# Token softmax in halves ahead of the state's reads, 1/rms spread by column transposes, and twelve weight products moved from GpSimd to VectorE

## The chip, the cores and the metric

The kernel runs on one core of a Trainium2 chip. The core has five engines with a queue each: TensorE (PE; its weight loads are listed apart as PEld), VectorE (DVE), ScalarE (ACT), GpSimd (POOL) and SyncE (SP), which issues most of the transfers. Each queue is worked off in order. The metric is the device time of one execution in microseconds; the kernel before takes 912.96 us (median of three runs, 911.79 to 913.95).

## The reference

The first part is a recurrent cross attention with B, H, S, Ns, D = 8, 8, 512, 32, 64; its result is reordered to 8 x 544 rows of 512 numbers. The second part is a SwiGLU feed-forward with d_ff = 1536, behind an RMS norm.

```python
scores = scale * np.matmul(x, state.transpose(0, 1, 3, 2))
scores = scores - scores.max(-1, keepdims=True)
a = np.exp(scores)
a /= a.sum(-1, keepdims=True) + 1e-09
xread = np.matmul(a, state)
# the same with scores2 = scale * state @ x^T gives sread = a2 @ x
return np.concatenate([xread, sread], axis=2).astype(np.float32)
...
rms = np.sqrt(np.mean(x * x, axis=-1, keepdims=True) + 1e-06)
xn = x / rms * rms_g
g = xn @ w_gate
silu = g * (1.0 / (1.0 + np.exp(-g)))
val = xn @ w_val
return (silu * val @ w_out).astype(np.float32)
```

The softmax over the 32 states, one for each token and head, is called the token softmax here; the one over the 512 tokens is the state softmax.

## The kernel before

**Weights.** The three matrices come as float64 and are made float32 on the chip, in 18 pieces of 1 MB: 12 of gate and val (pieces 0 to 11), 6 of w_out (12 to 17). `load_piece` loads a piece into one of four raw buffers, `to_float32` converts it in eight instructions: L151, L156, L157 and L159 on DVE, L153, L154 and L155 on ACT, and the last product, L162, on POOL. `ready(n)` asks for the first n pieces.

**Attention.** `attention(b)` is a generator that a `yield` cuts into 20 steps. For a batch it loads the state, transposes x (L209, copied by L210), makes the scores (L217), copies them to SBUF (L225), does the state softmax (L226 to L234), transposes its weights (L241) and reads x with them (L249), asks for the next batch's x (L258 and L87), then does the token softmax (L266 to L286), transposes its result (L294), and reads the state with it (L304) only to obtain the sum of squares for the norm (L307). `inverse_rms` raises that sum to the power -1/2 on POOL (L173, L175), and `along` spreads the result over the partitions: DVE multiplies it into a diagonal (L181), PE multiplies that by ones (L184). L311 scales the softmax weights by it. They lie in `aT_s`, the only thing of a token's read that is kept: `make_v` multiplies the state by the weights (L345, copied by L352), and the hidden layer then is `aT_s` by that product.

**Batch 0** is done with plain products: `hidden` (L371) for 12 blocks m, two for each pair of gate and val pieces, with L376 on ACT and L377 and L379 on DVE; then `project_as_ready` (L457), 48 products, four for each m, each pair of m needing one piece of w_out. Attention(1) runs a few steps at a time in between. Behind it `weight_sums` (L487) makes sums of w_out's blocks.

**Batches 1 to 7** use seven products in place of eight: `hidden_seven` (L409; L419, L421, L426 and L434 on ACT; L424, L428, L430, L435, L439, L444 and L446 on DVE) for six pairs, with two steps of attention(b+1) behind each pair, and `project_seven` (L500, copies L520, sums L525, and L533 and L542) with up to five steps at each of four places. In batch 7 the steps are those of `state_norm`, and 256 rows of state reads follow at the end.

**What sets the order.** The program is written in this order, and a scheduler then places the instructions of all queues by dependence and by its own costs, so the order on each engine can differ from that of the code. Buffers do the rest: PSUM tiles `at` (two), `f` and `pv`; in SBUF tiles with one tag share a place (`eS` with `e2T`, `sS` with `aT`, `xT0` with `e2`, `xT1` with `dg`).

Of the kernel before, what the change touches and what calls it, by code (L numbers as in the profile page):

```python
# [16 lines left out]
P = 128  # L17
# [4 lines left out]
def kernel(  # L22
# [61 lines left out]
    def load_x(b):  # L84
        x_sb[b] = one.tile([P, NC, H * D], F32, name="x_b")
        for c in range(NC):
            nc.sync.dma_start(  # L87
                out=x_sb[b][:, c].rearrange("p (h d) -> p h d", h=H),
                in_=x[b, :, P * c:P * c + P, :].rearrange("h p d -> p h d"))
# [50 lines left out]
    def to_float32(k):  # L140
# [3 lines left out]
        if k not in raw:  # L144
# [17 lines left out]
        GE.tensor_tensor(out=dst, in0=man.rearrange("p (a c f) -> p a c f", f=P, c=dst.shape[2]),  # L162
                         in1=ex.bitcast(F32).rearrange("p (a c f) -> p a c f", f=P, c=dst.shape[2]),
                         op=ALU.mult)
# [6 lines left out]
    def inverse_rms(ss, n):  # L171

        GE.tensor_scalar(ss, ss, 1.0 / DM, 1e-6, op0=ALU.mult, op1=ALU.add)  # L173
        ri = two.tile([P, NC], F32, name="ri")
        GE.tensor_tensor(out=ri[:, 0:n], in0=ss, in1=mhalf[:, 0:n], op=ALU.pow)  # L175
        return ri

    def along(ri, n):

        dg = one.tile([P, NC, P], F32, name="dg", tag="xT1")  # L180
        VE.tensor_tensor(out=dg[:, 0:n, :], in0=ident.unsqueeze(1).to_broadcast([P, n, P]),  # L181
                         in1=ri[:, 0:n].unsqueeze(2).to_broadcast([P, n, P]), op=ALU.mult)
        rp = aps.tile([P, S], F32, name="at")
        TE.matmul(out=rp[:, 0:n * P], lhsT=ones, rhs=dg[:, 0:n, :].rearrange("p c t -> p (c t)"),  # L184
                  start=True, stop=True)
        return rp

    def attention(b):
# [32 lines left out]
        e2 = one.tile([P, 2, NC, P], F32, name="e2", tag="xT0")  # L221
        m2 = two.tile([P, 2], F32, name="m2")
        z2 = two.tile([P, 2], F32, name="z2")
        for e in range(2):
            SE.copy(sS[:, e].rearrange("p c t -> p (c t)"), sp[e])  # L225
            VE.reduce_max(out=m2[:, e:e + 1], in_=sp[e], axis=AXX)  # L226
        yield

        VE.tensor_scalar(m2, m2, -SCALE, None, op0=ALU.mult)
        for e in range(2):  # L230
            SE.activation(out=e2[:, e], in_=sS[:, e], func=ACTF.Exp, scale=SCALE,  # L231
                          bias=m2[:, e:e + 1], accum_out=z2[:, e:e + 1])
        VE.tensor_scalar(z2, z2, 1e-9, None, op0=ALU.add)  # L233
        VE.reciprocal(z2, z2)  # L234
        yield

        e2T = one.tile([P, 2, NC, P], F32, name="e2T", tag="eS")
        for e in range(2):
# [4 lines left out]
            yield  # L243
        rp = aps.tile([P, 2, D], F32, name="at")
# [12 lines left out]
        if b + 1 < B:  # L257
            load_x(b + 1)  # L258
# [5 lines left out]

        eS = one.tile([P, NC, 2, 4, Ns], F32, name="eS", tag="eS")
        m1 = two.tile([P, NC * H], F32, name="m1")  # L266
        z1 = two.tile([P, NC, H], F32, name="z1")
        for cp in range(2):
            tp = aps.tile([P, 2, 2, P], F32, name="at")
            for c in range(2):  # L270
                for e in range(2):
                    TE.transpose(out=tp[:, c, e, :], in_=sS[:, e, 2 * cp + c, :], identity=ident)
            srows = tp.rearrange("p c e (j n) -> p (c e j) n", n=Ns)
            erows = eS[:, 2 * cp:2 * cp + 2].rearrange("p c e j n -> p (c e j) n")
            m = m1[:, 2 * H * cp:2 * H * cp + 2 * H]
            VE.reduce_max(out=m, in_=srows, axis=AXX)
            VE.tensor_tensor(out=erows, in0=srows, in1=m.unsqueeze(2).to_broadcast([P, 2 * H, Ns]),
                             op=ALU.subtract)
            SE.activation(out=erows, in_=erows, func=ACTF.Exp, scale=SCALE)
            yield  # L280
        z = z1.rearrange("p c h -> p (c h)")
        a = eS.rearrange("p c e j n -> p (c e j) n")
        VE.reduce_sum(out=z, in_=a, axis=AXX)
        VE.tensor_scalar(z, z, 1e-9, None, op0=ALU.add)
        VE.reciprocal(z, z)
        VE.tensor_tensor(out=a, in0=a, in1=z.unsqueeze(2).to_broadcast([P, NC * H, Ns]),  # L286
                         op=ALU.mult)
        yield

        aT = one.tile([P, 2, NC, P], F32, name="aT", tag="sS")  # L290
        for e in range(2):
            tp = aps.tile([P, NC, P], F32, name="at")
            for c in range(NC):
                TE.transpose(out=tp[:, c, :], in_=eS[:, c, e].rearrange("p j n -> p (j n)"),  # L294
                             identity=ident)
            SE.copy(aT[:, e], tp)
            yield


        ss = two.tile([P, NC], F32, name="ss")  # L300
        for c in range(NC):
            rp = aps.tile([P, 2, 4 * D], F32, name="at")
            for e in range(2):
                TE.matmul(out=rp[:, e, :], lhsT=aT[:, e, c, :],  # L304
                          rhs=bd[:, e].rearrange("p j d -> p (j d)"), start=True, stop=True)
            flat = rp.rearrange("p e f -> p (e f)")
            SE.activation(out=flat, in_=flat, func=ACTF.Square, accum_out=ss[:, c:c + 1])  # L307
            yield
        rp = along(inverse_rms(ss, NC), NC)
        aT_s[b] = two.tile([P, 2, S], F32, name="aT_s")  # L310
# [345 lines left out]
```

## Time and profile before

| | before |
|---|---|
| median of three runs | 912.96 us |
| the profiled execution | 913.43 us |
| its span on the core | 911.7 us |
| granted TensorE clock, mean | 0.979 |
| PE busy | 845.7 us (93%) |
| DVE busy | 474.2 us (52%) |
| ACT busy | 346.7 us (38%) |
| POOL busy | 212.0 us (23%) |

Busy time is a sum over the span and hides the stages, so the prediction reads it by stretches. A row of the timeline gives start and duration in us, the engine, the source line, the operation with its output and inputs, how many instructions it stands for, and in brackets how long the engine had been idle and what ended that. A row of a group gives the count, the busy time and the mean duration in ns of one, and then the idle time ahead of them. A row of the waits gives the total in us, the number of waits and the longest. In a row of the chain "issue" is time in which nothing was waited for that the profile shows.

### The profile page before, as it was taken

To read this page: it belongs to the slowest core of one execution; us is meant where nothing else is said; L and a number is where in the kernel's file an instruction comes from. 1 tells how busy PE (TensorE), PEld (TensorE's weight loads), DVE (VectorE), ACT (ScalarE), POOL (GpSimd) and SP (SyncE) were. 2 spreads that over 40 slices of the span, in tenths; PEclk is the share of its full clock that TensorE was granted. 3 is DMA by queue.
4 is the path that set the end of the run, shared out by engine and by line. 5 is a ranking of instruction groups with operands and counts; after the bars stand their busy time and mean duration, and the time that the engine had idled before them with its cause. 6 is when DMAs were issued, how large, how long until landed. Compare 5 with 4: busy or idle time off the path is not lost.

```text
span 911.7 us, 11827 instructions
## 1 busy us (share of the span) xinstructions
PE 845.7 (93%) x4726; PEld 621.0 (68%) x4726; DVE 474.2 (52%) x679; ACT 346.7 (38%) x600; POOL 212.0 (23%) x276
## 2 busy tenths in 40 slices
PE   3559779999999999999999999999999999999997
PEld 1234234467877787777787787778776877688886
DVE  4899996036822583167415761476246822571131
ACT  5765652246323642164315530563146322430110
POOL 2554430322122311222123203230323012310000
PEclk9869989999999999999999999999999999999999
DMA  9645302010201020102010011002000000000000
GB/s 272 195 144 167 130 28 47 0 50 1 47 12 36 3 47 1 47 4 47 0 42 8 18 30 35 12 1 47 24 24 1 2 16 31 1 1 24 24 1 23
DMA packets 53798, 37.46 MB, mean 41 GB/s; under 512 B 37872, under 2 KB 45552, under 8 KB 53744
## 3 DMA queue, kind: packets, MB, share of 16 engines
q1 hardware_dynamic: 53744, 36.71, 14.0%
q8 instruction: 37, 0.61, 0.3%
q14 instruction: 17, 0.14, 0.1%
HBM read 27.79 MB, written 8.91 MB: 40 GB/s over the span
## 4 chain that ended last, share of the span: by engine, by line
PE 66%; issue 16%; DVE 8%; ACT 4%; POOL 3%; DMA 1%; SPq 1%; ACTq 0%; DVEq 0%; POOLq 0%
PE f L500 22%; PE f L409 22%; PE pv L345 5%; PE f L371 5%; PE f L457 4%; PE at L304 2%; PE at L217 2%; PE at L209 2%; DVE ex L151 1%; PE at L184 1%; POOL ri L175 1%; DVE ex L159 1%; ACT e L231 1%; DVE dg L181 1%; DVE m L226 1%
## 5 line engine op out<-in xcount | busy, mean ns | idle before, releaser
L409 PE MATMUL f<-aT_s,v 128*128 128x256 f32 x504 | 132.6, 395 | 1.5 <-ACT g L426 1.5
L409 PEld LDWEIGHTS f<-aT_s,v 128*128 128x128 f32 x504 | 89.1, 190 | 51.5 <-issue 30.6
L500 PE MATMUL f<-wo,hb 128*128 128x256 f32 x540 | 121.6, 379 | 0.0
L500 PEld LDWEIGHTS f<-wo,hb 128*128 128x128 f32 x540 | 102.5, 190 | 16.7 <-issue 2.9
L352 ACT COPY v<-pv 128x512 f32<-128x512 f32 x96 | 51.7, 593 | 118.4 <-PE pv L345 118.4
L360 POOL TENSOR_TENSOR vs<-v 128x256 f32<-128x256 f32 x42 | 30.6, 729 | 271.1 <-ACT v L352 271.1
L409 PE MATMUL f<-aT_t,vs 128*128 128x256 f32 x336 | 86.4, 380 | 0.3 <-ACT g L419 0.3
L500 PE MATMUL f<-wt,hs 128*128 128x256 f32 x360 | 83.5, 382 | 0.0
L520 ACT COPY ot<-f 128x256 f32<-128x256 f32 x60 | 19.6, 375 | 163.1 <-PE f L500 163.1
L424 DVE TENSOR_TENSOR g<-g,f 128x512 f32<-128x512 f32 x42 | 28.9, 687 | 98.4 <-PE f L409 75.3
L500 PEld LDWEIGHTS f<-wt,hs 128*128 128x128 f32 x360 | 67.7, 190 | 10.3 <-DVE g L428 0.3
L409 PEld LDWEIGHTS f<-aT_t,vs 128*128 128x128 f32 x336 | 63.4, 190 | 9.8 <-issue 1.5
L345 PE MATMUL pv<-w,stT_g 64*32 64x512 f32 x768 | 65.7, 616 | 3.4 <-DVE z L233 1.9
L525 DVE TENSOR_TENSOR ot<-ot,f 128x256 f32<-128x256 f32 x45 | 17.1, 418 | 92.1 <-PE f L500 56.1
L434 ACT ACTIVATE hb<-g 128x1024 f32<-128x1024 f32 x42 | 44.4, 1057 | 44.6 <-DVE g L428 44.6
L371 PE MATMUL f<-aT_s,v 128*128 128x512 f32 x96 | 48.6, 662 | 9.1 <-DVE t L377 7.6
L435 DVE SCALAR_TENSOR_TENSOR hb<-hb,g 128x1024 f32<-128x1024 f32 x42 | 51.4, 1224 | 8.7 <-ACT hb L434 8.7
L200 POOL COPY bd<-rows 32x128 f32<-32x128 f32 x32 | 13.5, 423 | 150.5 <-PE at L304 148.8
L428 DVE TENSOR_TENSOR g<-g,f 128x512 f32<-128x512 f32 x42 | 28.9, 688 | 37.2 <-PE f L409 37.2
L371 PEld LDWEIGHTS f<-aT_s,v 128*128 128x128 f32 x96 | 19.4, 211 | 38.7 <-issue 19.7
L542 DVE TENSOR_TENSOR hs<-hb,hs 128x768 f32<-128x768 f32 x15 | 14.4, 959 | 59.5 <-PE f L500 59.5
L457 PE MATMUL f<-wo,hb 128*128 128x512 f32 x96 | 44.7, 612 | 0.0
(112 smaller groups left out, 1389.7 us busy)
## 6 DMA issues: line engine op xcount, KB each, us to landing
x_b<-in_x_dram SPq DMA_DIRECT2D x32, 256.0 KB, 4.6
out_dram<-ot SPq DMA_DIRECT2D x56, 128.0 KB, 1.8
raw<-in_moe_w_gate_dram SPq DMA_DIRECT2D x6, 1024.0 KB, 6.7
raw<-in_moe_w_val_dram SPq DMA_DIRECT2D x6, 1024.0 KB, 6.0
raw<-in_moe_w_out_dram SPq DMA_DIRECT2D x6, 1024.0 KB, 4.8
out_dram<-ot SPq DMA_DIRECT2D x4, 256.0 KB, 2.7
rows<-in_state_dram SPq DMA_DIRECT2D x32, 16.0 KB, 1.7
out_dram<-ot SPq DMA_DIRECT2D x16, 32.0 KB, 1.6
```

Of the source, the lines that this page charges most:

```text
L345: TE.matmul(out=pv[e][Ns * j:Ns * j + Ns, :], lhsT=stT_g[b][D * e:D * e + D, j, :], rhs=w[D * e:D * e + D, j, 2 * mp:2 * mp + 2].rearrange ...
L352: SE.copy(v[:, e].rearrange("p m k f -> p (m k f)"), pv[e])
L360: GE.tensor_tensor(out=vs[:, 0], in0=a21, in1=a22, op=ALU.add)
L371: TE.matmul(out=ps[:, 0:n], lhsT=lhs(i, k), rhs=r, start=(i == 0), stop=(i == len(rhs) - 1))
L409: TE.matmul(out=ps[:, i, :], lhsT=lhs[:, i, :], rhs=rhs, start=(start and i == 0), stop=True, skip_group_check=True)
L424: VE.tensor_tensor(out=g[:, :, 0, :], in0=g[:, :, 0, :], in1=ys, op=ALU.add)
L428: VE.tensor_tensor(out=g[:, :, 1, :], in0=g[:, :, 1, :], in1=zs, op=ALU.add)
L434: SE.activation(out=h, in_=gate, func=ACTF.Tanh, scale=0.5)
L435: VE.scalar_tensor_tensor(out=h, in0=h, scalar=1.0, in1=gate, op0=ALU.add, op1=ALU.mult)
L457: TE.matmul(out=op, lhsT=hb[:, m, P * r:P * r + P], rhs=wo[:, m, :], start=(m == 0), stop=(m == NM - 1))
L500: TE.matmul(out=ps[:, r, :], lhsT=lhs(k)[:, P * r:P * r + P], rhs=rhs(k), start=(start and r == 0 and k == 0), stop=(k == HM - 1), skip_gr ...
L520: SE.copy(kept[r], ps[:, r, :])
```

## The change

The edits:

1. x of batch 0 is asked for first, on ACT's queue; `rms_g` is loaded between piece 0 and piece 1.
2. The last product of the 12 gate and val pieces runs on DVE; the six of w_out stay on POOL.
3. `along` is gone. 1/DM is folded into the squares, the 1e-6 is added on DVE, the power stays on POOL, and PE transposes each column of the result, read 128 times over, into the place that the product with ones had.
4. The token softmax, its transposes, the reads for the norm and the scaling move ahead of the state softmax's transposes and reads. The sum, reciprocal and product of the token softmax are done in two halves. The maximum over tokens is taken from the scores' copy in SBUF. The next batch's x is asked for in the last step. There are 19 steps.

```diff
-    def load_x(b):
+    def load_x(b, queue):
...
-        GE.tensor_tensor(out=dst, in0=man.rearrange("p (a c f) -> p a c f", f=P, c=dst.shape[2]),
+        eng = VE if k < NM else GE
+        eng.tensor_tensor(out=dst, in0=man.rearrange("p (a c f) -> p a c f", f=P, c=dst.shape[2]),
...
-        GE.tensor_scalar(ss, ss, 1.0 / DM, 1e-6, op0=ALU.mult, op1=ALU.add)
+        VE.tensor_scalar(ss, ss, 1e-6, None, op0=ALU.add)
         ri = two.tile([P, NC], F32, name="ri")
         GE.tensor_tensor(out=ri[:, 0:n], in0=ss, in1=mhalf[:, 0:n], op=ALU.pow)
-        return ri
-
-    def along(ri, n):
...
+        rp = aps.tile([P, NC, P], F32, name="at")
+        for c in range(n):
+            TE.transpose(out=rp[:, c, :], in_=ri[:, c:c + 1].to_broadcast([P, P]), identity=ident)
+        return rp.rearrange("p c t -> p (c t)")
...
-            VE.reduce_max(out=m2[:, e:e + 1], in_=sp[e], axis=AXX)
+            VE.reduce_max(out=m2[:, e:e + 1], in_=sS[:, e].rearrange("p c t -> p (c t)"),
+                          axis=AXX)
+        yield
+
+        eS = one.tile([P, NC, 2, 4, Ns], F32, name="eS", tag="eS")
...
+        for cp in range(2):
+            tp = aps.tile([P, 2, 2, P], F32, name="at")
+            for c in range(2):
+                for e in range(2):
+                    TE.transpose(out=tp[:, c, e, :], in_=sS[:, e, 2 * cp + c, :], identity=ident)
...
+            VE.reduce_max(out=m, in_=srows, axis=AXX)
+            VE.tensor_tensor(out=a, in0=srows, in1=m.unsqueeze(2).to_broadcast([P, 2 * H, Ns]),
+                             op=ALU.subtract)
+            SE.activation(out=a, in_=a, func=ACTF.Exp, scale=SCALE)
+            yield
+
+        VE.tensor_scalar(s2, m2, -SCALE, None, op0=ALU.mult)
         for e in range(2):
             SE.activation(out=e2[:, e], in_=sS[:, e], func=ACTF.Exp, scale=SCALE,
...
+        aT = one.tile([P, 2, NC, P], F32, name="aT", tag="sS")
+        for cp in range(2):
...
+            VE.reduce_sum(out=z, in_=a, axis=AXX)
+            VE.tensor_scalar(z, z, 1e-9, None, op0=ALU.add)
+            VE.reciprocal(z, z)
+            VE.tensor_tensor(out=a, in0=a, in1=z.unsqueeze(2).to_broadcast([P, 2 * H, Ns]),
+                             op=ALU.mult)
...
+            SE.copy(aT[:, :, 2 * cp:2 * cp + 2, :].rearrange("p e c t -> p c e t"), tp)
+            yield
...
+            SE.activation(out=flat, in_=flat, func=ACTF.Square, scale=DM ** -0.5,
+                          accum_out=ss[:, c:c + 1])
+            yield
+        rp = inverse_rms(ss, NC)
...
+        VE.tensor_tensor(out=aT_s[b], in0=aT.rearrange("p e c t -> p e (c t)"),
+                         in1=rp.unsqueeze(1).to_broadcast([P, 2, S]), op=ALU.mult)
+        yield
...
         if b + 1 < B:
-            load_x(b + 1)
+            load_x(b + 1, nc.sync)
...
-        SE.activation(out=sq, in_=xsT, func=ACTF.Square)
+        SE.activation(out=sq, in_=xsT, func=ACTF.Square, scale=DM ** -0.5)
...
-        rp = along(inverse_rms(ss, NT // P), NT // P)
+        rp = inverse_rms(ss, NT // P)
...
+    load_x(0, nc.scalar)
     load_state(0)
     load_piece(0)
-    load_x(0)
+    nc.sync.dma_start(out=rms_g, in_=moe_rms_g.rearrange("(i p) -> p i", p=P))
     for k in range(1, RAW_AHEAD):
         load_piece(k)
```

Line numbers of the change are its own, a few lower than those of before. Three places show how the queues change.

On DVE, at the end of the conversions in batch 0, the last piece's passes stood before with the last two blocks of the hidden layer (L377, L379), and the weight sums (L487) followed:

```order
L159 SCALAR_TENSOR_TENSOR ex<-raw,ex 128x1024
L377 SCALAR_TENSOR_TENSOR t<-t,f 128x512
L151 TENSOR_SCALAR ex<-raw 128x1024
L379 SCALAR_TENSOR_TENSOR hb<-t,f 128x512
L156 TENSOR_SCALAR top<-raw 128x1024
L157 SCALAR_TENSOR_TENSOR raw<-top,raw 128x1024
L377 SCALAR_TENSOR_TENSOR t<-t,f 128x512
L159 SCALAR_TENSOR_TENSOR ex<-raw,ex 128x1024
L379 SCALAR_TENSOR_TENSOR hb<-t,f 128x512
L487 TENSOR_TENSOR wt<-wo 128x512 x2
```

Now all blocks of the hidden layer are done by then, and attention(1)'s softmax stands between the conversions of the last pieces of w_out (L157 and L159 are those of the last piece but one; the last piece follows this row group; L236, L237, L251 and L254 are the maximum, difference, sum and product of the token softmax):

```order
L221 TENSOR_REDUCE m_746<-sS 128x1 x2
L157 SCALAR_TENSOR_TENSOR raw<-top,raw 128x1024
L236 TENSOR_REDUCE m_753<-at 128x16 x2
L237 TENSOR_TENSOR eS<-at,m_753 128x512 x2
L242 TENSOR_SCALAR s_745<-m_746 128x2
L159 SCALAR_TENSOR_TENSOR ex<-raw,ex 128x1024
L251 TENSOR_REDUCE z_754<-eS 128x16 x2
L252 TENSOR_SCALAR z_754<-z_754 128x16
L290 TENSOR_SCALAR z_747<-z_747 128x2
L252 TENSOR_SCALAR z_754<-z_754 128x16
L253 RECIPROCAL z_754<-z_754 128x16 x2
L254 TENSOR_TENSOR eS<-eS,z_754 128x512 x2
```

The token softmax of attention(1) has moved from behind the weight sums to ahead of the last piece.

On PE, at the passage from batch 0's hidden layer (L371, now L368) to its output product (L457, now L454), the x transposes of attention(1) (L209) and its scores (L217) stood behind the last hidden block:

```order
L371 MATMUL f<-aT_s,v 128x512 x16
L209 MATMUL at<-ident,x_b 128x128 x8
L457 MATMUL f<-wo,hb 128x512
L209 MATMUL at<-ident,x_b 128x128 x8
L457 MATMUL f<-wo,hb 128x512 x7
L217 MATMUL at<-xT_681,stT 32x512 x4
L217 MATMUL at<-xT_682,stT 32x512 x4
L457 MATMUL f<-wo,hb 128x512 x4
L241 MATMUL at<-ident,e_738 128x128 x8
```

Now the transposes of x (L203) stand further up among the hidden blocks, and 18 output products stand ahead of the transposes of the normalised rows (L259), with the scores (L211) and the transposes of their copy (L232) between them:

```order
L342 MATMUL pv<-w,stT_g 32x512 x8
L211 MATMUL at<-xT_687,stT 32x512
L368 MATMUL f<-aT_s,v 128x512 x8
L454 MATMUL f<-wo,hb 128x512 x8
L211 MATMUL at<-xT_687,stT 32x512 x3
L211 MATMUL at<-xT_688,stT 32x512 x4
L454 MATMUL f<-wo,hb 128x512
L232 MATMUL at<-ident,sS 128x128
L454 MATMUL f<-wo,hb 128x512
L232 MATMUL at<-ident,sS 128x128 x7
L454 MATMUL f<-wo,hb 128x512 x8
L259 MATMUL at<-ident,eS 128x128 x8
```

The x transposes moved up by the last 16 hidden products and more, and the token softmax took the place of the state softmax.

On ACT, in the fifth and sixth pair of `hidden_seven` in batch 1, the copy of the xs product (L426) followed a copy of transposes (L242) and of `v`:

```order
L421 COPY c_1251<-f 128x512
L242 COPY e2T<-at 128x512
L352 COPY v<-pv 128x512 x2
L426 COPY g<-f 128x2x256
L434 ACTIVATE hb<-g 128x1024
```

Now a token exponential (L239) stands ahead of that copy (L423) and another ahead of the gate's tanh (L431):

```order
L418 COPY c_1264<-f 128x512
L349 COPY v<-pv 128x512 x2
L239 ACTIVATE eS<-eS 128x512
L423 COPY g<-f 128x2x256
L239 ACTIVATE eS<-eS 128x512
L431 ACTIVATE hb<-g 128x1024
```

Two exponentials moved up from `project_seven` into the pairs, each ahead of an instruction of the pair.

More of the change, by code (lines that the diff above doesn't have):

```diff
@@ L243, in attention @@
             yield
+        VE.tensor_scalar(z2, z2, 1e-9, None, op0=ALU.add)
+        VE.reciprocal(z2, z2)
         rp = aps.tile([P, 2, D], F32, name="at")
@@ L262, in attention @@
         yield
[L265 to L297, printed above, removed]
@@ L300, in attention @@
[L300 to L309, printed above, removed]
```

45 lines of the change are left out of this document (26 added, 19 removed).

## Prediction

> **What bounds the kernel now.** First the busy times by stretch, which show which engine each stage is limited by:
>
> ```profile
> 0.00:134.00 134.00, 88.02 (x352) 38.29 (x353) 116.56 (x118) 83.31 (x107) 56.44 (x44) 0.88 0.51 159
> 134.00:186.00 52.00, 50.10 (x228) 23.89 (x227) 17.52 (x30) 10.07 (x23) 9.71 (x15) 0.98 0.10 20
> ...
> 186.00:820.00 634.00, 620.53 (x3747) 482.98 (x3747) 319.16 (x482) 245.26 (x449) 145.84 (x218) 1.00 0.08 21
> ```
>
> The columns are the stretch, its length, then busy PE, PEld, DVE, ACT, POOL, the granted clock and DMA. Up to 134 us DVE is busy 116.6 us and PE only 88. From there on PE is busy 96 to 98%, so every later microsecond of PE work is on the path. Second, the chain of waits around the change of regime:
>
> ```profile
> 132.27 1.44 PE at L209 x8
> ...
> 147.52 1.03 PE at L249 x64
> ...
> 159.17 0.87 PE at L294 x8
> ...
> 160.91 3.71 PE at L304 x16
> ...
> 173.61 1.02 PE pv L345 x16
> 174.63 11.37 PE f L457 x26
> ...
> 186.02 0.59 ACT ot L461
> ```
>
> PE runs without a pause from 132.3 to 186.0 us: nearly all of batch 0's output product (L457) and all of attention(1) stand there. So the kernel is a DVE-bound front of about 133 us, a PE tail of batch 0 of 53.7 us, and a PE-bound rest. Third, what fills DVE in the front, from the timeline and from the groups:
>
> ```profile
> 112.46 2.40 POOL L162 TENSOR_TENSOR wo<-raw,ex 128x1024 f32<-128x1024 f32 x1 [1.16 <-DVE ex L159]
> 112.90 2.51 DVE L151 TENSOR_SCALAR ex<-raw 128x1024 int32<-128x1024 int32 x1
> ...
> 115.33 0.68 DVE L156 TENSOR_SCALAR top<-raw 128x1024 int32<-128x1024 int32 x1
> ...
> 115.93 0.68 DVE L151 TENSOR_SCALAR ex<-raw 128x1024 int32<-128x1024 int32 x1
> ...
> 116.53 1.21 DVE L157 SCALAR_TENSOR_TENSOR raw<-top,raw 128x1024 f32<-128x1024 int32 x1
> ...
> 117.67 0.67 DVE L377 SCALAR_TENSOR_TENSOR t<-t,f 128x512 f32<-128x512 f32 x1
> ...
> 118.27 1.21 DVE L159 SCALAR_TENSOR_TENSOR ex<-raw,ex 128x1024 int32<-128x1024 int32 x1
> ```
> ```profile
> L159 DVE SCALAR_TENSOR_TENSOR ex<-raw,ex 128x1024 int32<-128x1024 int32 x14 | 20.9, 1491 | 0.0
> L151 DVE TENSOR_SCALAR ex<-raw 128x1024 int32<-128x1024 int32 x13 | 18.3, 1405 | 0.0
> L157 DVE SCALAR_TENSOR_TENSOR raw<-top,raw 128x1024 f32<-128x1024 int32 x14 | 18.2, 1304 | 0.2
> L156 DVE TENSOR_SCALAR top<-raw 128x1024 int32<-128x1024 int32 x14 | 13.6, 970 | 0.0
> ...
> L286 DVE TENSOR_TENSOR eS<-eS,z 128x1024 f32<-128x1024 f32 x1 | 3.4, 3433 | 0.0
> ```
>
> The same L151 takes 2.51 us while POOL's product runs and 0.68 us when it doesn't: a product on POOL holds DVE up by 1.8 us. From 40 to 134 us (14 pieces) the four groups lie above their free durations (1.22, 0.68, 1.21, 0.68) by 3.8 + 9.4 + 1.3 + 4.1 = 18.6 us; L286, which is 1.22 us undisturbed (below), adds 2.2. That is 1.5 us for each product, and a few single instructions are held too. I take 1.6. Free prices from one start to the next: 0.60 us for L151, L156 and the 512-wide L377; 1.14 us for a 1024-wide pass with two inputs.
>
> **The change, part by part.** *The product of 12 pieces on VectorE.* Nearest rows for what it costs on DVE and what it cost on POOL:
>
> ```profile
> L286 DVE TENSOR_TENSOR eS<-eS,z 128x1024 f32<-128x1024 f32 x6 | 7.3, 1224 | 0.2
> ```
> ```profile
> L162 POOL TENSOR_TENSOR w<-raw,ex 128x1024 f32<-128x1024 f32 x12 | 30.7, 2557 | 49.0 <-DVE ex L159 45.0 <-issue 3.9
> ```
>
> DVE gains 12 x 1.14 = 13.7 us of work (at most 12 x 1.49 = 17.9, the contended mean of L159) and loses 12 stalls of 1.6 = 19.2 us (1.14 to 1.83 each). Net -5.5 us on DVE, between +4 and -8. POOL is cleared of 30.7 us and nobody waits for it there.
>
> The Trainium skill, SBUF — State Buffer, section "Who interferes with whom", says that DVE and GpSimd share one port pair under an exclusive lock, and that a DVE instruction with at most one SBUF input outside the two-port modes does not contend. By that rule the six products left on POOL hold up less where DVE reads PSUM; the trace agrees as far as L377 at 0.67 us, and the sum would fall by 1 or 2 us.
>
> *The order of attention.* The order now puts the token softmax of attention(1) into DVE's queue ahead of the last piece, and 18 of batch 0's 48 output matmuls, the x transposes and the scores ahead of that on PE. The one long wait I expect is PE's transposes of the normalised rows, which wait for DVE's second normalising product; call its end N. DVE's work up to N, from the 116.6 us above: one piece fewer, -(2 x 0.60 + 2 x 1.14 + 1.6) = -5.1; the products, -5.5; attention(1)'s part, ten 512-wide passes of 0.60 and some eight small ones of about 0.17, +7.4; no diagonal (L181), -0.6. Sum 112.8 us. DVE's idle time up to 134 us was 134.0 - 116.6 = 17.4 us; I take that and 2 us for the softmax's own latency, since its steps now follow each other in the queue. N = 112.8 + 19.4 = 132.2 us.
>
> Behind N PE still has 30 output matmuls of two instructions at 11.37/26 = 0.437 us, 26.2; the reads for the norm 3.7 (L304); two sets of eight transposes at 0.87 and four more at 0.11; L249 and L345, 1.03 and 1.02; a last transpose 0.1. Sum 34.3 us. Two short waits come on top. The sum of squares is now finished by a DVE instruction that stands behind the first weight sums, which wait for POOL's last piece; and the state read's scaling stands behind more of them. I give both together 2.5 us. Batch 0 ends at 132.2 + 34.3 + 2.5 = 169.0 us, against 186.0: **-17 us**.
>
> *The first loads.* x goes first on ACT's queue; before it stood behind the state and piece 0 on SP's, and held piece 1 up:
>
> ```profile
> 3.02 5.50 SPq L87 DMA_DIRECT2D x_b<-in_x_dram  x4
> ...
> 7.83 0.69 DVE L151 TENSOR_SCALAR ex<-raw 128x1024 int32<-128x1024 int32 x1 [7.83 <-DMA raw<-in_moe_w_gate_dram]
> ...
> 8.56 1.33 SPq L128 DMA_DIRECT2D raw<-in_moe_w_val_dram  x1
> ...
> 12.59 0.69 PE L209 MATMUL at<-ident,x_b 128*128 128x128 f32 x2 [0.43 <-DMA x_b<-in_x_dram]
> ...
> 18.41 1.07 ACT L225 COPY sS<-at 128x512 f32<-128x512 f32 x2 [1.03 <-PE at L217]
> ```
>
> x was complete at 12.6 us and the scores were copied at 18.4. Now x starts 2.3 us earlier but shares the engines with four pieces issued at once. ACT's and DVE's queues hold copies of x's transposes ahead of piece 0's last steps, so a late x stops the conversion too. I take no gain: bounds 10 us (start earlier by 2.3) and 19 us (behind all four pieces), or -3 to +6 us on N.
>
> The Trainium skill, DMA: Bandwidth & Descriptors, section "Queues, rings and completion order", says that each engine alternates between queue rows by packets of descriptors. x has 256-byte descriptors and the pieces 2 KB ones, so by that rule x would get the smaller share and land near the late bound; no run here has two queues loading at once, so it is a rival below.
>
> *The spread of 1/rms.* Per batch PE loses one L184 and gains four transposes. Before:
>
> ```profile
> 260.65 1.89 PE L500 MATMUL f<-wo,hb 128*128 128x256 f32 x8
> 260.88 1.33 POOL L200 COPY bd<-rows 32x128 f32<-32x128 f32 x4 [29.98 <-PE at L304]
> ...
> 262.57 1.02 POOL L175 TENSOR_TENSOR ri<-ss,mhalf 128x4 f32<-128x4 f32 x1
> ...
> 264.46 1.10 PE L184 MATMUL at<-dg,ones 128*128 128x512 f32 x2 [1.93 <-DVE dg L181]
> 265.40 0.81 PE L500 MATMUL f<-wo,hb 128*128 128x256 f32 x3
> ```
>
> L184 occupied PE for 0.94 us; four transposes at 0.11 are 0.44 (bound 0.94, if reading one column 128 times is slow): -0.5. The power still queues behind POOL's four block copies, so it ends about 0.25 + 1.33 + 1.05 = 2.6 us after the last read, without the diagonal's 0.8. But only three matmuls (1.3 us) instead of four stand between. Wait: 1.4 us with the semaphore, against 1.6 on average.
>
> ```profile
> PE at L184 <- DVE dg L181: 11.1, 7, 1.9
> PE f L409 <- ACT g L426: 1.5, 6, 0.2
> ```
>
> *A wait added in each batch.* In six batches ACT now has the first token exponential ahead of the copy of the xs product (L426), for which PE's next product waits. On DVE three more 512-wide passes stand ahead of it:
>
> ```profile
> 224.01 1.22 DVE L435 SCALAR_TENSOR_TENSOR hb<-hb,g 128x1024 f32<-128x1024 f32 x1 [0.20 <-ACT hb L434]
> ...
> 225.08 0.60 PE L241 MATMUL at<-ident,e 128*128 128x128 f32 x4
> ...
> 228.66 0.59 ACT L426 COPY g<-f 128x512 f32<-128x512 f32 x1 [0.74 <-PE f L409]
> ...
> 229.32 1.54 PE L409 MATMUL f<-aT_s,v 128*128 128x256 f32 x6
> ```
>
> From L435's start DVE needs 1.22 + six passes of 0.60 and a last one of 0.68 = 5.5 us, that is 4.4 after PE's transposes begin; the exponential 0.65 and the copy 0.6 end at 5.6. PE wants it at 229.32 - 225.08 + 0.44 (four transposes more) = 4.7. So 0.9 us against 0.25. Per batch -0.5 - 0.2 + 0.65 = 0: the rest of the kernel stays as it is. The rest I cost at nothing: the maximum of the scores read from their copy is the same 512-wide pass, the scale in the squares rides in an instruction that was there, and the sum and the reciprocal cut in two add about 0.5 us per batch to DVE, which is busy 319 us of 634. rms_g's 2 KB between pieces 0 and 1 delays piece 1 by one issue, 0.5 us, while ACT still waits for x; if x came first it would cost that 0.5 us. The later issue of x has cover: more than 20 matmuls of the output product (10 us) and two groups of the next batch, against a load that takes 5 us.
>
> **Sum.** 913.43 us (span 911.7 and 1.7 around it) - 17 + 0 = 896.4 us. The profiled execution lies 0.5 us above the median 912.96; I say **896.5 us**.
>
> **Rivals.** (1) *x comes late*: it lands at 19 us, N moves by +6, and PE, which then idles longer, runs some of its tail at the lower clock of the front (granted 0.88 up to 134 us, 0.98 behind it), another 2 us: 904.5. For it: one set of DMA engines, four pieces in flight. Chance 0.2. (2) *The front does not shrink*: the product on DVE costs as much as the stall it removes, and N slides by 13 us through ACT's latency, since ACT is busy 83 us of the front: 911. Against it: PE's 88 us of work leave room. Chance 0.06. (3) *The rest gains too*: if the exponential finds DVE free, the 0.65 is gone and the 1.4 us wait falls to nothing; 2 us in six batches: 884.5. Chance 0.09. (4) *Slower*: the softmax inside the hidden pairs makes PE wait in every batch, at the copy behind the exponential and at the transposes of the normalised rows, between which DVE has no slack. From 17/6 = 2.8 us per batch it decides; at 3.5 us the time is 896.5 + 21 = 917.5. Against it: PE idles only 634.0 - 620.5 = 13.5 us in the 634 us after batch 0 now, and DVE is busy half of that stretch. Chance 0.08.
>
> **How the numbers follow.** Forecast 0.57 (own range 890 to 902, from N's bounds of -3 to +4 and 0.5 us per batch). Range 885 to 909: it takes in rivals 1 and half of 3, and leaves out 2 and 4. A measurement tells about 0.2% (1.8 us) from no change: faster 0.87, same 0.05, slower 0.08.
>
> **What would show it.** DVE's product of the pieces at 1.2 us and few two-input passes over 2 us before the wo pieces; PE continuous from about 132 us with L457's successor half done; batch 0's last output copy near 169 us; x's landing in the first 20 us; the wait at the transposes of ri near 1.4 us and one at the xs product near 0.9, seven and six times. Wrong: a copy of the first output rows after 180 us, or PE idle over 4 us per batch after 200 us.

## The result, and the profile after

The changed kernel takes **891.63 us** (median of four executions, 888.89 to 892.65), against 912.84 us for the kernel before in the same runs: a ratio of 0.9763, 95% interval 0.9736 to 0.9789. The forecast was 896.5 us in a range of 885 to 909, and faster. The profiled execution of after took 888.89 us (span 887.1, mean granted clock 0.985); it is the fastest of the four.

The three stretches of the prediction in the kernel after (stretch, length, then busy PE, PEld, DVE, ACT, POOL, granted clock, DMA share, GB/s):

```profile
0.00:134.00 134.00, 95.20 (x413) 43.25 (x414) 111.44 (x147) 86.18 (x113) 23.05 (x30) 0.91 0.51 159
134.00:186.00 52.00, 49.09 (x257) 27.00 (x256) 20.30 (x32) 17.09 (x31) 16.26 (x19) 0.97 0.17 43
186.00:820.00 634.00, 624.31 (x3785) 492.68 (x3785) 317.14 (x506) 236.78 (x438) 144.97 (x207) 1.00 0.08 20
```

Up to 134 us DVE is busy 111.4 us instead of 116.6, although it now makes twelve products and attention(1)'s softmax in that stretch; PE got through 95 us of work instead of 88. The chain of waits at the change of regime, from the front that DVE limits to PE's work behind it (start, duration, engine, tile, line, count):

```profile
116.64 4.47 POOL wo L163
...
121.13 2.88 DVE ex L151
...
131.11 1.32 DVE z L252
...
132.86 0.60 DVE eS L254
...
133.60 1.96 PE at L259 x8
```

and, from the timeline, the copy of the first output rows (L461 at 186.02 us before):

```profile
170.15 0.59 ACT L458 COPY ot<-f 128x512 f32<-128x512 f32 x1 [10.23 <-PE f L454]
```

N, the end of the second normalising product, is 133.5 us (132.2 forecast), and batch 0 ends 15.9 us earlier (17 forecast). The span became 24.6 us shorter, so the **remaining 8.7 us were won behind batch 0**, where the forecast had none. Below, "front" is the start of the first output copy, "rest" the span less that: 186.0 and 725.7 us before, 170.2 and 716.9 after.

In the groups of DVE up to 190 us, and POOL's one, the products that are left on POOL show:

```profile
L159 DVE SCALAR_TENSOR_TENSOR ex<-raw,ex 128x1024 int32<-128x1024 int32 x18 | 22.0, 1222 | 3.4 <-ACT ex L154 3.4
L157 DVE SCALAR_TENSOR_TENSOR raw<-top,raw 128x1024 f32<-128x1024 int32 x18 | 22.0, 1220 | 0.0
L151 DVE TENSOR_SCALAR ex<-raw 128x1024 int32<-128x1024 int32 x18 | 16.4, 910 | 14.8 <-DMA raw<-in_moe_w_gate_dram 11.3 <-POOL wo L163 2.3 <-DMA raw<-in_moe_w_val_dram 1.1
L163 DVE TENSOR_TENSOR w<-raw,ex 128x1024 f32<-128x1024 f32 x12 | 14.6, 1218 | 0.0
L156 DVE TENSOR_SCALAR top<-raw 128x1024 int32<-128x1024 int32 x18 | 14.3, 810 | 0.0
```
```profile
L163 POOL TENSOR_TENSOR wo<-raw,ex 128x1024 f32<-128x1024 f32 x6 | 16.8, 2810 | 83.6 <-DVE ex L159 83.6
```

L157, L159 and the new L163 have their free durations (1.22 us) now. L151 and L156 still lie above theirs (0.69), and L151 waits 2.3 us for a buffer that POOL holds: POOL's mean is 2.81 us, because one of its six products took 4.47.

### The profile page after: what moved, and what is told of

Read it like the earlier page. It is cut to its first block, busy times and chain, and to the rows that moved or that the text cites. A ratio compares the mean times of both kernels' runs of the same rounds, so it can differ in the third digit from the quotient of the medians.

```text
span 887.1 us, 11884 instructions
## 1 busy us (share of the span) xinstructions
PE 831.5 (94%) x4742; PEld 618.0 (70%) x4742; DVE 465.7 (52%) x723; ACT 346.8 (39%) x600; POOL 184.3 (21%) x255
## 4 chain that ended last, share of the span: by engine, by line
PE 69%; issue 14%; DVE 7%; POOL 4%; ACT 3%; DMA 2%; POOLq 0%; ACTq 0%; DVEq 0%
PE f L497 26%; PE f L406 22%; PE f L368 7%; PE pv L342 5%; PE f L454 2%; DMA x_b<-in_x_dram 2%; PE at L270 1%; POOL wo L163 1%; PE at L203 1%; PE at L211 1%; ACT e L244 1%; DVE m L221 1%; PE at L297 1%; POOL ri L176 1%; PE at L287 1%
## 5 line engine op out<-in xcount | busy, mean ns | idle before, releaser
L406 PEld LDWEIGHTS f<-aT_s,v 128*128 128x128 f32 x504 | 89.4, 189 | 52.6 <-issue 29.8
L497 PE MATMUL f<-wo,hb 128*128 128x256 f32 x540 | 124.5, 382 | 0.0
L497 PEld LDWEIGHTS f<-wo,hb 128*128 128x128 f32 x540 | 100.6, 190 | 14.5 <-ACT ot L517 0.3
L522 DVE TENSOR_TENSOR ot<-ot,f 128x256 f32<-128x256 f32 x45 | 17.1, 418 | 100.1 <-PE f L497 64.3
L342 PE MATMUL pv<-w,stT_g 64*32 64x512 f32 x768 | 60.7, 599 | 0.6 <-DVE w L163 0.6
L431 ACT ACTIVATE hb<-g 128x1024 f32<-128x1024 f32 x42 | 44.4, 1057 | 33.1 <-DVE g L425 33.1
L368 PE MATMUL f<-aT_s,v 128*128 128x512 f32 x96 | 45.0, 621 | 3.1 <-ACT v L349 3.1
L454 PE MATMUL f<-wo,hb 128*128 128x512 f32 x96 | 44.6, 606 | 1.1 <-DVE hb L376 1.1
L406 PE MATMUL f<-aT_t,v 128*128 128x256 f32 x168 | 43.4, 380 | 0.0
L406 PE MATMUL f<-aT_s,vs 128*128 128x256 f32 x168 | 43.1, 379 | 0.0
L368 PE MATMUL f<-xsT,w 128*128 128x256 f32 x192 | 41.6, 379 | 0.0
```

The source lines that it names most:

```text
L342: TE.matmul(out=pv[e][Ns * j:Ns * j + Ns, :], lhsT=stT_g[b][D * e:D * e + D, j, :], rhs=w[D * e:D * e + D, j, 2 * mp:2 * mp + 2].rearrange ...
L368: TE.matmul(out=ps[:, 0:n], lhsT=lhs(i, k), rhs=r, start=(i == 0), stop=(i == len(rhs) - 1))
L406: TE.matmul(out=ps[:, i, :], lhsT=lhs[:, i, :], rhs=rhs, start=(start and i == 0), stop=True, skip_group_check=True)
L431: SE.activation(out=h, in_=gate, func=ACTF.Tanh, scale=0.5)
L454: TE.matmul(out=op, lhsT=hb[:, m, P * r:P * r + P], rhs=wo[:, m, :], start=(m == 0), stop=(m == NM - 1))
L497: TE.matmul(out=ps[:, r, :], lhsT=lhs(k)[:, P * r:P * r + P], rhs=rhs(k), start=(start and r == 0 and k == 0), stop=(k == HM - 1), skip_gr ...
```

## The experiments

All were timed beside the kernel before, whose median was 912.84 us beside the change and 911.5 to 911.7 us beside the others. Front and rest are from one execution of each kernel, the profiled one. Executions of one kernel mostly lie within 5 us of each other, at most 7.4 (895.88 to 903.28 us for the change with the old spread, whose profiled execution is the fastest), so a difference of 2 or 3 us between two single fronts shows little.

| kernel | median us | ratio to before, 95% | front | rest |
|---|---|---|---|---|
| before | 912.84 | | 186.0 | 725.7 |
| **the change** | 891.63 | 0.9763, 0.9736 to 0.9789 | 170.2 | 716.9 |
| before + products | 902.44 | 0.9896, 0.9881 to 0.9911 | 174.4 | 726.7 |
| before + order | 909.53 | 0.9970, 0.9960 to 0.9981 | 178.4 | 728.3 |
| before + spread | 903.32 | 0.9912, 0.9895 to 0.9930 | 185.1 | 716.4 |
| before + loads | 920.41 | 1.0080, 1.0056 to 1.0104 | 193.1 | 726.2 |
| change, products on POOL | 905.30 | 0.9931, 0.9910 to 0.9952 | 184.1 | 718.6 |
| change, old order | 896.90 | 0.9839, 0.9822 to 0.9857 | 177.6 | 716.9 |
| change, old spread | 898.84 | 0.9865, 0.9831 to 0.9898 | 169.9 | 724.2 |
| change, old loads | 890.48 | 0.9770, 0.9749 to 0.9792 | 173.1 | 718.6 |
| change, x on SP's queue | 889.06 | 0.9750, 0.9727 to 0.9773 | 168.9 | 718.3 |
| change + idle products on POOL | 912.06 | 1.0003, 0.9991 to 1.0014 | 190.3 | 717.0 |
| change, all 18 products on DVE | 882.80 | 0.9681, 0.9664 to 0.9697 | 163.9 | 717.2 |
| both of the above for x and products | **881.62** | 0.9666, 0.9651 to 0.9680 | 160.8 | 719.9 |

### One edit alone in the kernel before

The theory: products and order shorten the front, the spread and the loads do little. The rival: the loads or the rest decide.

**Products** of the 12 gate and val pieces on VectorE:

```diff
-        GE.tensor_tensor(out=dst, ...
+        eng = VE if k < NM else GE
+        eng.tensor_tensor(out=dst, ...
```


> The kernel before with the 12 gate and val products on VectorE, nothing else. If the stall theory holds (a product on GpSimd holds VectorE up by 1.6 us, on VectorE it costs 1.14), batch 0 ends about 5.5 us earlier (first output copy at 180 to 181 us in place of 186.0) and the rest keeps its length: 907 us. If the move pays only together with the new order, the time stays within 2 us of 912.8. Two-input passes over 2 us on VectorE should remain only for the six w_out products.

Measured: 902.44 us, better than the 907 of the theory; the front is 11.7 us shorter and the rest 1.0 us longer. That is more than the 5.5 us that the sum has for DVE's queue. The chain shows where the remainder came from. Before, PE's x transposes of attention(1) stood at the passage (L209, 132.27 us) and its scores at 141.11 us. With this edit alone the passage reads:

```profile
129.62 1.14 DVE raw L157
130.76 1.21 DVE m L227 x2
...
133.06 1.97 PE at L242 x8
```

What PE waits for at 133.06 us is already the state softmax; the transposes of x and the scores are done by then. So are 24 instructions of batch 0's output product, where before only 2 stood ahead of the passage (timelines of PE, 110 to 133 us). At 0.437 us each the 22 are 9.6 us; with the transposes (1.44 us) and the scores (1.02) that is 12.1 us of PE's work ahead of the passage, though the order in the code is the old one.

**Order** of attention's steps (the whole of `attention` as in the change, with the old spread; the diff is an outline in words):

```diff
     scores
+    token softmax in halves, its transposes, reads, scaling
     state softmax's transposes and reads
-    token softmax, its transposes, reads, scaling
```


> The kernel before with the new order of attention alone (token softmax first, in halves, next x asked for last), the old spread by a diagonal and ones, old loads, products on GpSimd. Theory: the front gains because output products and attention(1) move under VectorE's work; the transposes of the normalised rows in attention(1) wait until about 138 us, batch 0 ends near 176 us (-10), the rest loses or gains under 1 us per batch: 902 to 904 us. Rival, that the product's move carries the gain: no change, 911 to 914.

Measured: 909.53 us, where 902 to 904 had been expected: the front is 7.6 us shorter instead of 10, and the rest 2.6 us longer.

**Spread** of 1/rms by column transposes:

```diff
-        VE.tensor_tensor(out=dg[:, 0:n, :], in0=ident ..., in1=ri ..., op=ALU.mult)
-        TE.matmul(out=rp, lhsT=ones, rhs=dg, start=True, stop=True)
+        for c in range(n):
+            TE.transpose(out=rp[:, c, :], in_=ri[:, c:c + 1].to_broadcast([P, P]), identity=ident)
```


> The kernel before with only the column transposes in place of the diagonal and the product with ones (1/DM in the squares, 1e-6 added on VectorE). Theory: 0.9 us per batch after batch 0 (0.5 of PE work, 0.4 of wait) and about 2 us in the front, where the diagonal took 2.9 us on VectorE under a GpSimd product: 904 to 907 us. Rival: the wait for the power stays and only 0.5 us per batch goes: 909.

Measured: 903.32 us, at the lower end of what was expected, with the front 0.9 us and **the rest 9.3 us shorter**: the whole gain of the rest, from an edit that the forecast had at -0.7 us per batch and cancelled against a wait.

**Loads** in the new order:

```diff
+    load_x(0, nc.scalar)
     load_state(0)
     load_piece(0)
-    load_x(0)
+    nc.sync.dma_start(out=rms_g, ...)
```


> The kernel before with only the new loads (x of batch 0 on ScalarE's queue, rms_g after piece 0). x should land at 15 us in place of 12.6, as in the changed kernel, and piece 0 at 11 in place of 7.8. Theory: no gain, 0 to +3 us (913 to 916), since VectorE starts later and is the bound. Rival, that the earlier start of x is part of the gain: 910 or less.

Measured: 920.41 us, 0.8% slower than before and slower than the 913 to 916 expected, nearly all of it in the front (+7.1 us). This edit costs time by itself. So of the theory the products and the order hold, but the spread gives almost as much as the products, and the loads cost.

### One edit taken out of the change

The same four, undone one at a time, tell whether they add up. The first three use the lines of before for the part named.

```diff
-        eng = VE if k < NM else GE
+        eng = GE
```


> The changed kernel with all 18 products on GpSimd again. Stall theory: 12 times 0.46 us back on VectorE, the transposes of the normalised rows wait until about 139 us in place of 133.6, 896 to 898 us. If the product is the core of the gain: over 903.

> The changed kernel with the old order of attention. Theory: the output products of batch 0 and attention(1) return behind VectorE's work, batch 0 ends near 178 to 180 us in place of 170.2: 899 to 902 us. Rival (order is worth nothing): 891 to 893.

> The changed kernel with the diagonal and the product with ones again. Theory: 0.9 us per batch back and about 1 us in the front: 898 to 900 us. Rival: 0.5 us per batch, 895.

Measured: 905.30, 896.90 and 898.84 us. The first is a miss of the stall theory (896 to 898): the products are the largest part of the gain. The second lies between theory and rival, the third is as expected. In the front the products are worth 13.9 us inside the change (11.7 alone), the order 7.4 (7.6 alone), the spread nothing either way (0.3 and 0.9). In the rest the spread is worth 7.3 us (9.3 alone). So in the front these three edits nearly add up. The four front effects found alone sum to -11.7 - 7.6 - 0.9 + 7.1 = -13.1 us, against -15.9 in the change. In the rest they don't add up: the order costs 2.6 us alone and nothing inside the change, and the four effects found alone sum to 1.0 + 2.6 - 9.3 + 0.5 = -5.2 us, against -8.7. What removes the order's cost there is open.

### The first loads in the change

The new order once with x back on SP's queue, behind the state and ahead of piece 0, and once with all loads as before:

```diff
-    load_x(0, nc.scalar)
     load_state(0)
+    load_x(0, nc.sync)
     load_piece(0)
```


> The changed kernel with x of batch 0 on SyncE's queue, behind the state and ahead of piece 0, so that it shares the engines with nothing. x should land near 8 or 9 us in place of 15.3 and piece 0 near 11. Theory, that x's late landing holds ScalarE's and VectorE's queues up: the front shortens by 3 to 5 us, 887 to 889. Rival, that piece 0's landing is the limit: no change, 891 to 893.

```diff
-    load_x(0, nc.scalar)
     load_state(0)
     load_piece(0)
-    nc.sync.dma_start(out=rms_g, ...)
+    load_x(0, nc.sync)
     for k in range(1, RAW_AHEAD):
         load_piece(k)
+    nc.sync.dma_start(out=rms_g, ...)
```


> The changed kernel with the first loads in the order of the kernel before (state, piece 0, x, pieces 1 to 3 and rms_g, all on one queue). If two queues at once make x and piece 0 late, x lands near 12.6 us and piece 0 near 7.8 us again, the conversion starts 3 us earlier and batch 0 ends 3 to 7 us earlier: 885 to 889 us. If the front of the change is no longer bound by the loads: 890 to 893 us.

Measured: 889.06 and 890.48 us; both intervals overlap that of the change. So the first does not decide between its theory and its rival, and the second gives its rival's time. The landings, from the timeline of after, and then of the kernel with x on SP's queue:

```profile
0.74 3.77 ACTq L87 DMA_DIRECT2D x_b<-in_x_dram  x4
...
11.34 0.69 DVE L151 TENSOR_SCALAR ex<-raw 128x1024 int32<-128x1024 int32 x1 [11.34 <-DMA raw<-in_moe_w_gate_dram]
...
15.27 3.12 PE L203 MATMUL at<-ident,x_b 128*128 128x128 f32 x13 [3.37 <-DMA x_b<-in_x_dram]
```
```profile
2.56 2.85 SPq L87 DMA_DIRECT2D x_b<-in_x_dram  x4
...
9.35 0.29 PEld L203 LDWEIGHTS at<-ident,x_b 128*128 128x128 f32 x2 [0.42 <-DMA x_b<-in_x_dram]
...
12.54 0.69 DVE L151 TENSOR_SCALAR ex<-raw 128x1024 int32<-128x1024 int32 x1 [7.93 <-DMA raw<-in_moe_w_gate_dram]
```

Issued first, on a queue of its own, x was complete at 15.3 us. Issued 1.8 us later on the queue that also carries the weights, but ahead of them, it was complete at 9.4. And piece 0 landed at 11.3 us in the change, against 7.8 before: with two queues at once both were late. With x on SP's queue piece 0 came later still, at 12.5 us, and the kernel isn't slower for it. The old loads bring piece 0 back to 7.9 us, and still the time is within the change's. In that run the granted clock was lower afterwards (windows of after, then of the change with the old loads):

```profile
20.00:40.00 20.00, 11.51 (x63) 6.58 (x48) 19.67 (x32) 17.30 (x29) 4.04 (x7) 0.74 0.36 112
40.00:60.00 20.00, 17.55 (x115) 8.39 (x116) 14.18 (x19) 10.95 (x16) 1.57 (x3) 0.83 0.70 194
```
```profile
20.00:40.00 20.00, 13.67 (x46) 6.39 (x44) 17.13 (x29) 14.54 (x24) 1.15 (x4) 0.66 0.44 133
40.00:60.00 20.00, 16.05 (x109) 7.81 (x110) 13.44 (x18) 11.96 (x16) 2.91 (x5) 0.74 0.53 142
60.00:80.00 20.00, 19.96 (x77) 8.13 (x76) 20.00 (x26) 15.40 (x20) 0.00 (x0) 1.00 0.61 209
```

The clock was 0.66 and 0.74 where after had 0.74 and 0.83, and from 60 to 80 us PE was busy throughout, 19.96 us against 18.43 in after, with DVE at 20.00 us in both. That the clock ate the earlier start is a reading of these rows and not shown: no run varied the clock alone, and the profiled execution with the old loads is the slowest of its four (893.46 us; the others took 889.40 to 891.52).

### Is it POOL's hold on DVE, or POOL's latency?

The products could have cost time in two ways: because POOL, while it makes one, holds DVE up (the theory), or because the hidden layer gets its weights later from a slower engine (the rival). This kernel keeps the product on DVE and lets POOL make it once more, into a buffer that is read by nobody (the output is as before; the instructions in the queues shift somewhat with it):

```diff
+        if k < NM:
+            GE.tensor_tensor(out=top.bitcast(F32), in0=man, in1=ex.bitcast(F32), op=ALU.mult)
```


> The changed kernel, in which POOL also makes each of the 12 products of gate and val pieces once more, into a buffer that nobody reads (it replaces the piece's top words). So nothing waits for POOL's product, but POOL is as busy as before the change. If the product on POOL cost what it cost because it held DVE up (1.14 to 1.83 us each on DVE, 14 to 22 us in all), that comes back on top of DVE's own products: 904 to 913 us. If it cost because the hidden layer waited for POOL's slower result, nothing of it comes back but buffers that come free up to 2.5 us later: 890 to 895 us.

Measured: **912.06 us**; the front is 20.2 us longer, the rest the same. In its groups (DVE, then POOL, up to 190 us):

```profile
L163 DVE TENSOR_TENSOR w<-raw,ex 128x1024 f32<-128x1024 f32 x12 | 28.0, 2333 | 0.1
L159 DVE SCALAR_TENSOR_TENSOR ex<-raw,ex 128x1024 int32<-128x1024 int32 x18 | 23.8, 1325 | 4.7 <-ACT ex L154 4.7
L157 DVE SCALAR_TENSOR_TENSOR raw<-top,raw 128x1024 f32<-128x1024 int32 x18 | 23.7, 1318 | 0.1
...
L156 DVE TENSOR_SCALAR top<-raw 128x1024 int32<-128x1024 int32 x18 | 14.5, 815 | 2.3 <-POOL top L167 2.3
```
```profile
L167 POOL TENSOR_TENSOR top<-raw,ex 128x1024 f32<-128x1024 f32 x12 | 36.0, 3000 | 67.1 <-DVE ex L159 61.5 <-issue 5.6
```

Nobody reads POOL's result, yet DVE's twelve products take 28.0 us instead of 14.6, and L159, L157 and L156 another 3.7 together. These 17.1 us are **1.4 us for each product on POOL**, inside the forecast's 1.14 to 1.83 and near the 1.6 taken. The remaining 3 us of the front are about what DVE's waits show: 2.3 us for the buffer that POOL is writing, and 1.3 us more for ACT. Since nothing waits for POOL's values, latency of the weights isn't the cause of these 20 us.

The hold doesn't make up all that the products were worth, though. With the products on POOL inside the change (905.30 us), L151, L156, L157 and L159 take 91.6 us of DVE up to 190 us, against 74.7 in after: 16.9 us, again 1.4 for each product. DVE's own products cost 14.6, so on DVE's queue the move is worth 2.3 us of the 13.9. The waits up to 190 us in that kernel, then in after, show the rival at work as well:

```profile
PE pv L342 <- POOL w L163: 22.4, 6, 7.6
DVE ex L151 <- POOL w L163: 4.6, 2, 2.3
```
```profile
PE pv L342 <- DVE w L163: 0.6, 1, 0.6
```

PE waits for POOL's values there, and DVE for buffers that POOL holds. How much of the other 11.6 us is due to these waits, and how much to the queues' changed order, no run separates.

### All products on VectorE, and the best version

```diff
-        eng = VE if k < NM else GE
+        eng = VE
```


> The changed kernel with the product of the six w_out pieces on DVE as well. By the forecast's terms each costs DVE 1.14 us and frees it of 1.6 us: six times -0.5 us, 2.8 us, and the last piece's product, for which the weight sums wait at 139.7 to 142.2 us, takes 1.2 instead of 2.4 us: 886.5 to 889 us. If the six products on POOL lie mostly beside passes that they don't hold up, DVE, which is the bound of the front, gets up to 6 x 1.14 = 6.8 us more: 893 to 898 us.

Measured: **882.80 us**, better than expected: the front is 6.3 us shorter once more, and the profiled executions differ by 6.0 us. From the timeline of after, then of this kernel, the stretch ahead of N:

```profile
116.44 1.25 DVE L157 SCALAR_TENSOR_TENSOR raw<-top,raw 128x1024 f32<-128x1024 int32 x1
116.64 6.82 POOL L163 TENSOR_TENSOR wo<-raw,ex 128x1024 f32<-128x1024 f32 x2 [5.36 <-DVE ex L159]
...
117.58 1.25 DVE L159 SCALAR_TENSOR_TENSOR ex<-raw,ex 128x1024 int32<-128x1024 int32 x1
...
121.13 2.88 DVE L151 TENSOR_SCALAR ex<-raw 128x1024 int32<-128x1024 int32 x1 [2.31 <-POOL wo L163]
...
130.00 2.40 POOL L163 TENSOR_TENSOR wo<-raw,ex 128x1024 f32<-128x1024 f32 x1 [6.54 <-DVE ex L159]
...
131.04 1.39 DVE L252 TENSOR_SCALAR z<-z 128x16 f32<-128x16 f32 x1
...
132.78 1.28 DVE L254 TENSOR_TENSOR eS<-eS,z 128x512 f32<-128x512 f32 x2
```
```profile
124.86 1.23 DVE L163 TENSOR_TENSOR wo<-raw,ex 128x1024 f32<-128x1024 f32 x1
...
127.18 0.17 DVE L252 TENSOR_SCALAR z<-z 128x16 f32<-128x16 f32 x1
...
127.70 1.28 DVE L254 TENSOR_TENSOR eS<-eS,z 128x512 f32<-128x512 f32 x2
```

In after, DVE waits 2.31 us for a buffer that a product of POOL holds, its L151 then takes 2.88 us beside the next product, and a tiny L252 takes 1.39 us beside the last one, against 0.17. All three are gone, and the two normalising products start at 127.70 us instead of 132.78. The expectation had counted a stall of 1.6 us for each product, but not the wait for the buffer. What the six products held up, 7.1 us (added up below), is about what they cost on DVE, 7.3 us; so most of the gain lies in such waits: the 2.31 us here, and 2.5 us for which the weight sums in after wait for POOL's last product.

Both improvements together, that is x on SP's queue ahead of piece 0 and all products on DVE:

> Both edits that may beat the change: x of batch 0 on the same queue as the state, ahead of piece 0, and all 18 products on DVE. If the two gains add up (2 us from x, 3 to 5 us from the products): 884 to 887 us. If the products on DVE cost more than they free: 890 to 896 us, as the kernel with all products on DVE but about 2 us less.

Measured: **881.62 us**, 0.9666 of before (0.9651 to 0.9680), below the 884 to 887 expected: faster than before, and than the change, whose interval begins at 0.9736. It isn't told apart from all products on DVE alone (0.9664 to 0.9697): its front is 3.1 us shorter, its rest 2.7 us longer.

## Why the prediction was right, point by point

**What bounds the kernel: right.** A front bound by DVE, then PE (in the kernel before not quite "without a pause": ahead of 168.22 us PE waits 1.90 us for the diagonal). N came out 1.3 us and batch 0's end 1.1 us behind the forecast. Of the 36.7 us between them, 34.3 + 2.5 = 36.8 had been forecast, and the two short waits are the two that were named: 1.1 us at the spread and 1.8 us at the state read. What set the end was partly DVE again, behind POOL's last product, as the chain of after shows:

```profile
139.73 2.41 POOL wo L163
142.17 1.43 DVE wt L484 x2
...
147.47 1.13 DVE aT_s L278
...
153.44 4.29 PE f L454 x10
```

**The products: the hold right, their worth too small.** A hold of 1.6 us was taken, 1.4 us measured by the idle products. The six left on POOL held L151 and L156 up by 4.0 + 1.9 us against the kernel with all products on DVE (12.4 us in each group there) and L252 by 1.2: also 1.2 us each. The rule cited from the Trainium skill, SBUF — State Buffer, section "Who interferes with whom", had let expect 1 or 2 us less for these six; against 1.4 us each it is about 1. The row that the prediction gave for the rule, L377 at 117.67 us, lies between two products of POOL (112.46 to 114.86, and 119.56 us) and shows nothing. The same trace has a fitting one: L377, whose second input lies in PSUM, took 0.69 us at 80.84 us, inside a product that ran from 80.24 to 82.66 us.

"Net -5.5 us on DVE, between +4 and -8" was meant as what the products are worth. They were worth 11.7 us of the front alone and 13.9 inside the change, beyond that bound. The sum had the hold alone; inside the change the waits for POOL's values and buffers come on top (above), alone PE had more of its later work done ahead of the passage, and how much each makes is open. N came out well all the same, in part by errors that cancel. Up to 134 us DVE was busy 111.4 us, where the sum had 112.8 up to N. Its idle time there was 22.6 us, where 19.4 was taken, and the difference is the next point.

**The first loads: inside the bounds, on their late side.** "I take no gain" was mild. x landed at 15.3 us, between the forecast's 10 and 19, and piece 0 at 11.3 instead of 7.8, of which the forecast had nothing: DVE's wait for gate pieces grew from 7.8 to 11.3 us. The rule cited from the Trainium skill, DMA: Bandwidth & Descriptors, section "Queues, rings and completion order", gave the right direction: x, in 256-byte descriptors on a queue of its own, was complete 6 us later than on one queue ahead of the pieces. Rival 1's 19 us did not occur. Alone the loads cost 7.1 us of front, in the change the old loads (0.9770) can't be told from the new (0.9763). With the loads alone, DVE waits 10.8 us for its first piece against 7.8 before, and 4.6 us for buffers that POOL's products of gate and val hold, where before has no such wait; in the change those products are on DVE. That this is the reason is not shown.

**The order: right in the front, its added wait mis-sized.** It brought 7.4 to 7.6 us to the front. The wait that it adds in each batch was put at 0.9 us against 0.25. In after, in batch 1:

```profile
211.86 0.68 DVE L237 TENSOR_TENSOR eS<-at,m 128x512 f32<-128x512 f32 x1
...
212.58 0.63 ACT L239 ACTIVATE eS<-eS 128x512 f32<-128x512 f32 x1 [0.65 <-DVE eS L237]
...
213.11 0.57 ACT L423 COPY g<-f 128x512 f32<-128x512 f32 x1
...
213.73 1.99 PE L406 MATMUL f<-aT_s,v 128*128 128x256 f32 x8 [0.23 <-ACT g L423]
```

The exponential does stand ahead of the copy, and PE does wait for that copy, but 0.23 us: from the start of the earlier 1024-wide pass (207.59 us) DVE needed 1.26 + five passes of 0.60 + 0.68 = 4.95 us, not 5.5. One pass fewer stood ahead than was counted.

**The spread: mis-sized.** The step that failed is "Per batch -0.5 - 0.2 + 0.65 = 0". The waits of PE behind 160 us in after, to set beside the prediction's rows (11.1 us and 1.5 us):

```profile
PE at L179 <- POOL ri L176: 7.1, 7, 1.3
PE f L406 <- ACT g L423: 2.6, 11, 0.2
```

The work on PE is as forecast: four transposes take 0.48 us, from 239.40 to 239.88 us in batch 1, instead of 0.94, so reading one column 128 times is not slow. The wait fell from 11.1 / 7 = 1.59 to 7.1 / 7 = 1.01 us, by 0.57 and not 0.2. The xs copy added (2.6 - 1.5) / 7 = 0.16, not 0.65. The sum is -0.46 - 0.57 + 0.16 = -0.87 us per batch; from batch 1's spread to batch 6's, five batches take 471.89 us against 476.28, 0.88 us less each. Six batches, and 1.3 us at the norm of the state reads (its wait 0.26 us instead of 0.80, its step on PE 0.36 instead of 1.08), make 6.6 of the 8.7 us. Another 1.6 us were won behind that norm, in the last stretch; it appears with the spread alone and also in the change with the old spread, and its cause is open. The remaining 0.5 us are not placed.

**The rivals.** Rival 3 gave the right place but half the reason: the 0.65 nearly vanished, the 1.4 us wait did not fall to nothing. Rivals 2 and 4 did not come about. The forecast landed 4.9 us high because a gain of 8.7 us in the rest was put at nothing, while the front gained 1.1 us less and the median lies 2.7 us above the profiled run.

## What to carry to other kernels

Price an engine that shares something with the bottleneck by what it does to the bottleneck: twelve products, 30.7 us of work on a POOL that was busy 56 of the first 134 us, were worth 11.7 to 13.9 us of the front, and six more another 6. Count both its hold on the other engine and the waits for its values and its buffers: the hold alone, less what the products cost on DVE, comes to 2.3 us here. A term that recurs in every batch deserves as much care as the large one-time term: two errors of 0.4 and 0.5 us per batch, on two waits, made most of the difference here. And a bundle can hide a part that loses: the load order was 0.8% slower by itself, which only the single edits showed.

## What the runs showed of the hardware that was not expected

- The hold goes both ways. A product of 2.40 us on POOL took 4.47 while DVE ran L157 and L159 beside it in 1.25 us each. The Trainium skill, SBUF — State Buffer, section "Who interferes with whom", says that whichever of the two issues first blocks the other for its whole instruction; this trace agrees for L157, which started 0.2 us ahead of the product, and the prediction had used only one direction. L159 started 0.9 us behind the product's recorded start and still ran its free time, so the product seems to have waited for both passes: 2.07 us more than 2.40 is more than what was left of L157.
- A short DVE instruction is held to the end of POOL's product as a large one is: a 128x16 one took 1.39 us beside a product, up to 132.43 us where the product ended at 132.40, and 0.17 us without.
- A load that started 1.8 us sooner, on a second queue, was complete 6 us later: x at 15.3 us instead of 9.4.
- The granted clock early in the front differs between kernels that differ by a few microseconds of their start: 0.74 and 0.83, or 0.66 and 0.74, in the windows from 20 to 60 us, in one execution of each. In these two, a first piece that came 3.4 us sooner was not found again at the end of the front (170.2 and 173.1 us).
